# Merging the two parity halves of each K and V transfer into one, in a layer of sliding dilated attention and SwiGLU

## The chip, the cores and the metric

One core of a Trainium2 chip runs the whole layer. The metric is device time in microseconds; the time of a kernel is the median of its runs. A profiled execution gives the rows that are read here. Engines: PE multiplies matrices, DVE (VectorE) does most elementwise work, ACT (ScalarE) copies, scales and applies functions, POOL (GpSimd) does next to nothing here, and SP issues the transfers (DMA), which run on 16 DMA engines.

## The reference

A transformer layer on one sequence of S = 2048 positions, D = 640 channels, float32, with 32 heads of 20 channels. Each position attends to 8 positions of the past, two apart.

```
h  = x  + attention(layernorm(x), wqkv, wo)
h2 = h  + (silu(layernorm(h) @ w_gate) * (layernorm(h) @ w_up)) @ w_down      # F = 1728
...
# attention
W, dil = 8, 2
idx  = pos[:, None] - dil * arange(W)[None, :]        # the positions a query sees
kg   = k[:, :, idx, :] ;  vg = v[:, :, idx, :]
logits = einsum("bhsd,bhswd->bhsw", q, kg) * Dh ** -0.5   # masked where idx < 0
o    = einsum("bhsw,bhswd->bhsd", softmax(logits), vg)
```

## The kernel before

The sequence is cut into 4 blocks of 512 positions (b) and the heads into 4 groups of 8 heads, 160 channels (g). A pair (b, g) is a unit; there are 16. Because a query sees every second position only, positions of even and odd parity never meet in the attention. The 128 partitions hold it so: partitions 0 to 63 are one parity, 64 to 127 the other, and each partition owns 4 neighbouring positions of its parity.

The work of a unit:

- `qkv(b, g)` computes Q, K and V on PE into PSUM banks (L696). ACT evicts them (L703) into the staging tile `st`.
- SP stores them to DRAM: K to `ksc`, V to `vsc`, Q to `qsc`. `ksc` and `vsc` have the shape [4 groups, 2 parities, 1031 rows, 160]; a row is a position of one parity, and the first 7 rows are a halo of zeros, written once at the start by `zero_halo` (L460). Each of K and V is stored in two transfers (`put`, L716), one for each parity, from 64 partitions each.
- `att_load(b, g)` loads them again, so that each partition gets its own 4 positions and the 7 before them: 11 rows, 1760 elements, 7040 bytes, overlapping with its neighbour's. Each of K and V is loaded in two transfers (`ld`, L752), one for each parity, to 64 partitions each, into one of three slots of the tile `kv`, in turn: K of unit 0, V of unit 0, K of unit 1 and so on.
- DVE multiplies Q by the windows of K (L767) and reduces (L773); after the softmax it multiplies by the windows of V (L808), adds up (L817) and transposes (L824). The result is stored to `osc` in small transfers (L830).

Beside the attention of later units, PE computes the output projection (L901) and the feed-forward layer of earlier blocks (L989, L1004; L1158 and L1405 in the last blocks, where products are shared between blocks). The FFN weights come from DRAM (L951, L980), are split by ACT (L970) and DVE (L965) into a high and a low part, since each product is made in three passes, and the low parts are stored in the first block and loaded again in later ones (`lsc`, L980 and L975).

All steps are listed with `P.add(engine, cost, function, reads, writes, ...)`, and their order on each engine is written out as a table, `ORDER`, of (engine, first step, count). Waits follow from what each step reads and writes: a step waits for the steps that wrote what it reads, and for those that still use what it overwrites. All transfers but eight are issued by SP, one after the other in the order of the table; a transfer whose data isn't ready holds up those behind it. The names of the reads and writes of K and V carry the parity: `K{g}{par}` in DRAM and `fakv{par}` in the tile.

Of the kernel before, what the change touches and what calls it, by code (L numbers as in the profile page):

```python
# [19 lines left out]
NB, NJ, NG, NC = 4, 4, 4, 5  # L20
GC = D // NG
# [298 lines left out]
def nb(chunks, size):  # L320
    return (chunks / 16 * 0.042 + chunks * size / 435e3) * RATE
# [1286 lines left out]
```

## Time and profile before

| what | us |
|---|---|
| median of 3 runs | 842.3 |
| the runs | 841.67, 842.3, 843.37 |
| the profiled execution's own time | 845.17 |
| its span, first to last instruction | 843.4 |
| PE busy | 835.2 (99%) |
| DVE busy | 744.5 (88%) |
| ACT busy | 426.3 (51%) |

The page of the profile gives the busy time of each engine, then the span in 40 slices with the busy share of each in tenths; PEclk is PE's granted clock and DMA the mean share of the 16 DMA engines that is busy. Rows of transfers name target and source, the number of issues, the size of one and the median time from its issue to its landing. A row of a tile's answer gives the duration of an instruction (least, median, greatest, in ns; for SP it is the issue alone) and the first and last start in us. In a row of a stage the first figure is the stage's length, then comes each engine's busy time, the granted clock, the DMA share and the GB/s moved.

### The profile page before, as it was taken

The numbers are of one execution on the slowest core, as the hardware profiler recorded it, in microseconds if no ns is written. First come the engines' busy times: TensorE is split into PE (matmuls) and PEld (weight loads), VectorE is DVE, ScalarE is ACT, GpSimd is POOL, SyncE is SP. The second block draws the span as 40 slices with busy tenths as digits, with TensorE's granted clock in tenths as the row PEclk, the third lists the DMA queues.
The fourth block names the chain that finished last, engine by engine and source line by source line (L and its number), as shares of the span: only waits on it lengthen the run. The fifth ranks groups of instructions, "written<-read, shape, count | busy, mean of one in ns | idle before, by whom it ended". The sixth has DMA issues, their size and how long they took to land. (4 is left out here: it accounts for less than half of the span.)

```text
span 843.4 us, 11052 instructions
## 1 busy us (share of the span) xinstructions
PE 835.2 (99%) x4049; PEld 717.4 (85%) x4049; DVE 744.5 (88%) x934; ACT 426.3 (51%) x774; POOL 3.4 (0%) x14
## 2 busy tenths in 40 slices
PE   8999999999999999999999999999999999999998
PEld 7888888889888888888888888888888888888998
DVE  6599999999999999999999999996797676576996
ACT  7966476244873343567345347554464323335451
POOL 0000000000000000000000000000000000000000
PEclk9999999999999999999999999999999999999999
DMA  7988977678788898877999989977522133475002
GB/s 250 261 214 239 271 177 195 186 209 234 175 246 250 270 272 289 229 237 234 299 288 304 261 242 270 257 281 274 167 78 100 57 113 100 156 256 222 0 33 93
DMA packets 89877, 174.88 MB, mean 207 GB/s; under 512 B 33744, under 2 KB 53200, under 8 KB 89056
## 3 DMA queue, kind: packets, MB, share of 16 engines
q1 hardware_dynamic: 88416, 173.53, 67.7%
q10 hardware_dynamic: 1408, 0.66, 0.3%
q8 instruction: 31, 0.51, 0.2%
q14 instruction: 22, 0.18, 0.1%
HBM read 126.04 MB, written 46.80 MB: 205 GB/s over the span
## 5 line engine op out<-in xcount | busy, mean ns | idle before, releaser
L989 PE MATMUL bank<-shb,rb 128*128 128x512 f32 x930 | 227.0, 390 | 1.4 <-DVE fa L1028 0.7
L989 PEld LDWEIGHTS bank<-shb,rb 128*128 128x128 f32 x930 | 173.2, 188 | 38.4 <-DVE fa L1028 2.1
L1004 PE MATMUL bank<-rb,acts 128*128 128x512 f32 x464 | 121.4, 391 | 0.0
L1004 PEld LDWEIGHTS bank<-rb,acts 128*128 128x128 f32 x464 | 86.4, 188 | 17.3
L767 DVE TENSOR_TENSOR pq<-kv,pq 128x2560 f32<-128x2560 f32 x32 | 90.2, 2819 | 3.2 <-DMA pq<-qsc 1.9
L817 DVE TENSOR_TENSOR pq<-pq 128x1280 f32<-128x1280 f32 (+2 forms) x96 | 89.6, 934 | 2.2
L808 DVE TENSOR_TENSOR pq<-kv,pq 128x2560 f32<-128x2560 f32 x32 | 90.3, 2821 | 1.3 <-DMA kv<-vsc 0.7
L773 DVE TENSOR_REDUCE pq<-pq 128x128 f32<-128x2560 f32 x32 | 90.1, 2814 | 0.2
L703 ACT ACTIVATE st<-bank,fa 128x480 f32<-128x480 f32 (+3 forms) x120 | 50.4, 475 | 43.2 <-PE bank L696 40.8
L901 PE MATMUL bank<-ra 128*128 128x320 f32 x360 | 55.9, 309 | 0.9 <-ACT fa L904 0.9
L901 PEld LDWEIGHTS bank<-ra 128*128 128x128 f32 x360 | 54.2, 188 | 2.7 <-ACT fa L904 1.3
L970 ACT CAST rb<-fa 128x1280 fp32r<-128x1280 f32 (+1 forms) x35 | 42.5, 1217 | 25.2 <-DMA fa<-in_ffn_dram 20.0
L696 PE MATMUL bank<-ra,sha 128*128 128x480 f32 (+2 forms) x240 | 53.6, 380 | 0.0
L696 PE MATMUL bank<-rb,sha 128*128 128x512 f32 (+1 forms) x240 | 52.6, 378 | 0.0
L696 PE MATMUL bank<-ra,shb 128*128 128x512 f32 (+1 forms) x240 | 52.0, 378 | 0.0
L696 PE MATMUL bank<-rb,shb 128*128 128x512 f32 (+1 forms) x230 | 50.8, 379 | 0.0
L696 PEld LDWEIGHTS bank<-ra,shb 128*128 128x128 f32 x240 | 45.0, 188 | 6.5
L696 PEld LDWEIGHTS bank<-rb,sha 128*128 128x128 f32 x240 | 44.9, 188 | 6.4
L696 PEld LDWEIGHTS bank<-ra,sha 128*128 128x128 f32 x240 | 44.5, 188 | 6.6 <-ACT sha L643 0.2
L696 PEld LDWEIGHTS bank<-rb,shb 128*128 128x128 f32 x230 | 42.9, 188 | 6.3
L965 DVE TENSOR_TENSOR rb<-fa,rb 128x640 fp32r<-128x640 f32 (+1 forms) x54 | 43.4, 818 | 1.3 <-DMA lsc<-rb 0.7
L1027 ACT ACTIVATE fa<-bank 128x512 f32<-128x512 f32 x34 | 20.3, 598 | 42.4 <-PE bank L989 38.4
(211 smaller groups left out, 1264.8 us busy)
## 6 DMA issues: line engine op xcount, KB each, us to landing
fa<-in_ffn_dram SPq DMA_DIRECT2D x35, 960.0 KB, 7.1
kv<-ksc SPq DMA_DIRECT2D x32, 440.0 KB, 6.7
kv<-vsc SPq DMA_DIRECT2D x32, 440.0 KB, 7.4
rb<-lsc SPq DMA_DIRECT2D x17, 640.0 KB, 5.8
lsc<-rb SPq DMA_DIRECT2D x13, 640.0 KB, 6.0
rb<-lsc SPq DMA_DIRECT2D x19, 320.0 KB, 6.8
ksc<-st SPq DMA_DIRECT2D x32, 160.0 KB, 3.7
vsc<-st SPq DMA_DIRECT2D x32, 160.0 KB, 3.1
```

The costliest lines, as they stand in the source:

```text
L696: T.matmul(banks[bk][:, 0:n], l, r_(wq(g, w, c) + shift, n), start=(p, c) == first_mm, stop=(p, c) == last_mm)
L703: P.add("ACT", act(m) + 0.06, lambda: A.activation(stage_t()[:, o : o + NJ * m].rearrange("p (t j c) -> p t j c", j=NJ, c=w)[:, :, j, :], ...
L767: P.add("DVE", dve(2560), lambda: V.tensor_tensor(pq(PROD, 2560).rearrange("p (j w c) -> p j w c", j=2, w=W), window(ko, 2 * jp), pq(qo + ...
L773: P.add("DVE", dve(2560), lambda: V.tensor_reduce(logits(lo)[:, :, 16 * jp : 16 * jp + 16].rearrange("p h n -> p n h"), pq(PROD, 2560).rea ...
L808: V.tensor_tensor(pq(PROD, 2560).rearrange("p (j n d) -> p j n d", j=2, d=DH), bass.AP(tensor=v.tensor, offset=v.offset, ap=[list(v.ap[0]) ...
L817: V.tensor_add(dst(v), v[:, :, 0:m, :], v[:, :, m : 2 * m, :])
L901: T.matmul(banks[bk][:, 0:320], l, r_(m, 320), start=p == 0 and c == 0, stop=p == 2 and c == NC - 1)
L965: low(640, lambda E, o=o: E.tensor_sub(ws(t, lo + o, 640)[p0:], fa[p0:, raw + o : raw + o + 640], ws(t, hi + o, 640)[p0:].bitcast(F32)), [ ...
L970: P.add("ACT", act(n), lambda: A.copy(ws(wt, gu, n), f(raw, n)), r=[rf(raw, n)], w=[rws(wt, gu, n)], prio=PR["fh"])
L989: T.matmul(banks[bk], ws(wt, gu + 1280 * w + wid * c + col, 128), x(a, c), start=p == 0 and c == 0, stop=p == 2 and c == NC - 1)
L1004: T.matmul(banks[k], l, m, start=first and p == 0, stop=stop and p == len(passes) - 1)
L1027: P.add("ACT", act(512), lambda: A.activation(f(so, 512), banks[5], AF.Silu), r=[pb(5)], w=[rf(so, 512)], prio=0, table="silu")
```

## The change

Each of a unit's K and V is stored in one transfer from all 128 partitions, and loaded in one to all 128. The pattern in DRAM then has the parity as its first dimension, of size 2, ahead of the 64 partitions of a parity. The names of reads and writes lose the parity in DRAM, and a load writes both halves of its slot. The bytes moved, the rows (2560 bytes in a store, 7040 in a load) and all arithmetic stay as they are.

```
-            def put(par, dst, o):
+            def put(dst, o):
                 Q.dma_start(
-                    dst[g, par, 7 + 256 * b : 7 + 256 * b + 256, :].rearrange("(r j) c -> r (j c)", j=NJ),
-                    stage_t()[64 * par : 64 * par + 64, o : o + 640],
+                    dst[g, :, 7 + 256 * b : 7 + 256 * b + 256, :].rearrange("a (r j) c -> a r (j c)", j=NJ),
+                    stage_t()[:, o : o + 640],
                 )
...
-                for par in range(2):
-                    P.add("SP", 0.65, lambda par=par, dst=dst, o=o: put(par, dst, o), r=[("ab", o, o + 640)],
-                          w=[(f"{nmd}{g}{par}", 1000 + 256 * b, 1256 + 256 * b)], prio=PR["kvs"], nbytes=nb(64, 2560))
+                P.add("SP", 0.65, lambda dst=dst, o=o: put(dst, o), r=[("ab", o, o + 640)],
+                      w=[(f"{nmd}{g}", 1000 + 256 * b, 1256 + 256 * b)], prio=PR["kvs"], nbytes=nb(128, 2560))
...
-                for par in range(2):
-                    def ld(dst=dst, o=o, par=par):
-                        a = dst[g, par, 256 * b, :]
-                        Q.dma_start(kv_t()[64 * par : 64 * par + 64, o : o + 1760],
-                                    bass.AP(tensor=a.tensor, offset=a.offset, ap=[[640, 64], [1, 1760]]))
-                    lo_r = 0 if b == 0 else 1000 + 256 * (b - 1)
-                    P.add("SP", 0.45, ld, r=[(f"{nmd}{g}{par}", lo_r, 1000 + 256 * (b + 1))], w=[(f"fakv{par}", o, o + 1760)], prio=PR["atl"], nbytes=nb(64, 7040))
+                def ld(dst=dst, o=o):
+                    a = dst[g, 0, 256 * b, :]
+                    Q.dma_start(kv_t()[:, o : o + 1760],
+                                bass.AP(tensor=a.tensor, offset=a.offset, ap=[[SEQ * GC, 2], [640, 64], [1, 1760]]))
+                lo_r = 0 if b == 0 else 1000 + 256 * (b - 1)
+                P.add("SP", 0.45, ld, r=[(f"{nmd}{g}", lo_r, 1000 + 256 * (b + 1))], w=[("fakv0", o, o + 1760), ("fakv1", o, o + 1760)], prio=PR["atl"], nbytes=nb(128, 7040))
```

The table `ORDER` is written anew. It lists the same steps for PE (816), DVE (857), ACT (633) and POOL (41), in another order on each; SP has 487 steps instead of 551. The loads of K and V come at about the same places among PE's steps: the last one, V of the last unit, after 432 of PE's 816 steps instead of 433. In some units of blocks 2 and 3 the K of the next unit is loaded ahead of the V of this one.

More of the change, by code (lines that the diff above doesn't have):

```diff
@@ L467, in program @@
                 "SP", 0.07, lambda t=t: zero_halo(t), r=[rpq(PROD, 1120)],
-                w=[(f"{nm}{g}{a}", 0, 7) for g in range(NG) for a in range(2)], prio=6, nbytes=36e3,
+                w=[(f"{nm}{g}", 0, 7) for g in range(NG)], prio=6, nbytes=36e3,
             )
```

452 rows, old and new, of the table ORDER are left out of this document.

## The prediction

> **What bounds the kernel now.** I read the page first, for its shares and its DMA table, then the tiles that the change moves, then the engines and the DMA by stage, and last the count of DMA packets at the start.
>
> ```profile
> span 843.4 us, 11052 instructions
> PE 835.2 (99%) x4049; PEld 717.4 (85%) x4049; DVE 744.5 (88%) x934; ACT 426.3 (51%) x774; POOL 3.4 (0%) x14
> PEclk9999999999999999999999999999999999999999
> DMA  7988977678788898877999989977522133475002
> ...
> kv<-ksc SPq DMA_DIRECT2D x32, 440.0 KB, 6.7
> kv<-vsc SPq DMA_DIRECT2D x32, 440.0 KB, 7.4
> rb<-lsc SPq DMA_DIRECT2D x17, 640.0 KB, 5.8
> ...
> ksc<-st SPq DMA_DIRECT2D x32, 160.0 KB, 3.7
> vsc<-st SPq DMA_DIRECT2D x32, 160.0 KB, 3.1
> ```
>
> PE is busy 835.2 of 843.4 us at an undiminished granted clock, so PE sets the time, and a change of the transfers can win no more than the other 8.2 us. It can lose much more: the DMA engines are busy in seven to nine tenths of most slices of the first two thirds.
>
> The answers for the tiles kv and ksc show where the K and V transfers lie (first and last start), and the engines by stage show what else goes on there.
>
> ```profile
> L752 SPq DMA_DIRECT2D kv<-ksc x32: 445/492/988, 27.7 to 504.2; - x32
> L752 SPq DMA_DIRECT2D kv<-vsc x32: 444/462/934, 40.4 to 521.5; - x32
> L716 SPq DMA_DIRECT2D ksc<-st x32: 445/524/1482, 24.5 to 247.5; - x32
> ```
>
> ```profile
> core 0: us, PE busy (x) PEld busy (x) DVE busy (x) ACT busy (x) POOL busy (x), PEclk, DMA share, GB/s
> 24.00:250.00 226.00, 226.00 (x1117) 199.18 (x1116) 213.67 (x212) 137.67 (x299) 0.00 (x0) 1.00 0.81 220
> 250.00:542.00 292.00, 289.72 (x1367) 243.62 (x1366) 284.65 (x296) 144.47 (x220) 0.73 (x2) 1.00 0.87 264
> 542.00:843.40 301.40, 297.83 (x1476) 256.47 (x1474) 231.46 (x391) 127.51 (x219) 1.51 (x5) 1.00 0.40 140
> ```
>
> From 24 to 542 us all 64 loads and all 64 stores of K and V are made. PE loses 2.3 us in that stage (292.00 less 289.72), and DVE, which does the attention, is busy 498 of 518 us. In all this the transfers stay hidden. After 542 us no K or V moves, and the change touches nothing but the order.
>
> **What the change does to one transfer.** Of 128 issues 64 go: 32 loads and 32 stores. By the rows above an issue holds the SP queue some 0.46 to 0.56 us, so SP gains about 64 x 0.51 = 33 us. SP's issues are on no path; SP stands and waits for others, as the row below has it, so I cost this at nothing (if that cover were gone, the gain would still be bounded by PE's 2.3 us).
>
> ```profile
> SPq L830 <- DVE pq L824: 47.2, 16, 5.8
> ```
>
> What counts is the form of what is left. Before, a load reads 64 rows for 64 partitions: the pattern in DRAM starts with a dimension of 64. After, the DRAM pattern starts with the parity, a dimension of 2, with 64 rows inside, against 128 partitions in SBUF. The two parities lie 1031 x 160 elements apart, 64 rows only 64 x 640 (or, for the store, the same), so the dimensions cannot fold into one of 128. Nothing in the trace of before starts with a 2. The smallest are the two halo stores (L460), which start with 8. The start of the run, as far as 23.4 and 23.5 us, shows on how many engines one of these ran:
>
> ```profile
> GB/s 0 0 0 105 337 385 394 309 222 335 372 385 392 396 379 434 414 279 53 118 203 328 171 33 128 259 179 158 420 350 438 403 245 89 142 154 387 253 109 57
> DMA packets 3003, 5.74 MB, mean 245 GB/s; under 512 B 1064, under 2 KB 2098, under 8 KB 2874
> ...
> fa<-in_wqkv_dram SPq DMA_DIRECT2D x4, 480.0 KB, 4.2
> fa<-in_wqkv_dram SPq DMA_DIRECT2D x7, 240.0 KB, 5.3
> fa<-in_x_dram SPq DMA_DIRECT2D x4, 320.0 KB, 3.3
> fa<-in_x_dram SPq DMA_DIRECT2D x1, 1280.0 KB
> fa<-in_wqkv_dram SPq DMA_DIRECT2D x2, 32.0 KB, 3.3
> vsc<-pq SPq DMA_DIRECT2D x1, 35.0 KB
> ksc<-pq SPq DMA_DIRECT2D x1, 35.0 KB
> fa<-in_const_dram SPq DMA_DIRECT2D x1, 16.0 KB, 5.7
> fa<-in_wqkv_dram SPq DMA_DIRECT2D x1, 16.0 KB, 2.3
> ```
>
> ```profile
> DMA packets 3008, 5.75 MB, mean 245 GB/s; under 512 B 1064, under 2 KB 2103, under 8 KB 2879
> ```
>
> ```profile
> q10 hardware_dynamic: 1408, 0.66, 0.3%
> kv<-fa ACTq DMA_DIRECT2D x8, 80.0 KB, 2.8
> ```
>
> The last fence is the key to the count: 8 transfers of 80 KB in rows of 512 bytes are 1280 packets, and 128 more are counted, 16 for each transfer: one small packet at each engine's end. At the start, the rows below 512 bytes are the 32 KB, 32 KB, 16 KB and 16 KB transfers in rows of 128 bytes, 768 packets. Of the 1064 small packets 296 are left, and that is 18 x 16 + 8 (the number does not move between 23.4 and 23.5 us, so no transfer is halfway through its ends; three of the 22 issued have yet to finish). The transfer that starts with 8 ended on 8 engines, the others on 16. I read it so: the engines of a transfer follow the size of its outermost dimension. With a 2 ahead on the DRAM side that gives two engines, each with 64 rows. The trace allows the other reading too (the engines follow the number of rows, 128 here, and all 16 work); that is the second rival.
>
> [...]
>
> **The sum with two engines.** A whole load has 128 x 7040 = 901,120 bytes (twice the 440 KB), 450,560 on each of the two; a whole store 327,680, 163,840 on each. What does one engine carry? In the row of GB/s above, the best slices reach 434 and 438, or 27 GB/s for each of 16. The mean over the stage is lower:
>
> ```profile
> DMA packets 66211, 126.89 MB, mean 245 GB/s; under 512 B 28756, under 2 KB 41594, under 8 KB 65666
> ...
> q1 hardware_dynamic: 66178, 126.46, 84.2%
> ```
>
> That is 24 to 542 us: 245 / 16 / 0.845 (with the instruction queues' share) = 18.1 GB/s for an engine while it is busy. I take 26 for K and V: when two engines carry, the other 14 stand, and nothing competes with them, so they are nearest to the best slices. A load is then 17.3 us on both engines (16.7 at 27, 24.9 at 18.1), a store 6.3 us (6.1; 9.1). 16 units with two loads and two stores each: 16 x (34.6 + 12.6) = 755 us (728; 1086).
>
> The other transfers of the stage still run over all 16 and stand in the same queues: 126.46 MB less 28.8 (loads) and 10.5 (stores) is 87.1 MB, 5.45 MB for each engine: 202 us at 27 GB/s, 301 at 18.1, since many of them are small rows; I take the middle, 251. So the two engines have 755 + 251 = 1006 us of work in a stage that lasts 518 us now. PE's 516 us in it no longer cover that. The stage becomes DMA bound, and grows by at least 488 us if the two engines never stand idle.
>
> They will: SP issues in order, and each K load waits for the DVE to be done with the V two loads back, each store for ACT. Now the DMA engines stand 15.5% of the stage. With the same share after, the stage is 1006 / 0.845 = 1191 us, 673 more. A deeper queue at the two engines lets SP run further ahead than now, so I take the middle of 488 and 673, 580 us.
>
> Against the profiled execution, 845.2 us (1.8 beyond its span): 845 + 580 = 1425. It stands 2.9 us above the median of the runs, so 1422 for a median; I say **1420 us**. The low end, all at 27 GB/s and no idle time: 728 + 202 = 930, 412 more, 1257. The high end, all at 18.1 and no idle time: 1086 + 301 = 1387, 869 more, 1714. What is late next: a weight load that stands in line behind a K load comes 17 us later at two of its 16 engines, so PE and DVE wait for FFN weights as much as for K and V. After 542 us I take PE's 301 us as they are.
>
> **What could go otherwise.**
> 1. *The waiting PE slows down as well.* All slices show a granted clock of 1.00, because PE is never idle for long. Half fed, it need not keep that. At half clock its 516 us in the stage would be 1031, as much as the two engines' work, and two queues of about the same length that wait for each other would not overlap fully: if a fifth of the shorter stuck out (my guess), some 200 us more, 1620. Nothing in the rows of before speaks for it or against it, as PE nowhere starves. [...]
> 2. *All 16 engines carry the merged transfers.* For it: every transfer of 128 partitions here runs on 16. Then the change helps the DMA: a half load of 440 KB takes 6.7 us to land, one of 640 KB on 128 partitions (rb<-lsc above) 5.8, so halves are slow for their bytes and a whole of 880 KB might land in some 8 us instead of two times 6.7 in a row. But PE has only 2.3 us to win in the stage. Half of it won: 842.3 - 1.2 = 841 us, which is within the 0.2% (1.7 us) that the spread of the three runs, 841.67 to 843.37, can tell from no change; all of it won, with some of the 3.6 us after 542, 839 us. [...] This is the case on the other side, and it decides if the landing of a K load stays below about 9 us.
> 3. *All 16 engines, but a wait too coarse.* The load of a unit's K now waits for both halves of the store and for both halves of the buffer, and DVE for the last row of 128. If each of 32 loads came 0.5 us later to a DVE that is busy 98% of the stage, it would be 16 us, 858 us. Against it: the loads are issued well ahead, as PE's idle time shows.
>
> **Chances.** Two engines, as summed: 0.75. Two engines with a slow PE: 0.11. 16 engines and a little gain or none: 0.11 (0.07 within 0.2%, 0.04 faster). 16 engines and coarse waits: 0.03. So slower 0.89, same 0.07, faster 0.04. The first two cases together lie between 1257 and 1714, rounded to 1250 and 1720, with about 0.95 of their 0.86; the rest, 0.18, lies outside. As cases of the other sign hold little, this is also the likeliest one's range.
>
> **What would show it.** Two engines: K and V loads as x16 with 880 KB, landing in 19 us or more (17.3 and what stands ahead), stores as x16 with 320 KB in over 7 us; the mean DMA share of the stage down to about (2 x 1006 + 14 x 251) / 16 / 1100 = 0.31 while the stage doubles; PE busy near 59% of the span with the same busy time; waits of DVE for kv<-ksc and kv<-vsc, and of ACT for the FFN weights, on top of the list; and fewer small packets, as each of the 64 transfers ends on 2 engines. A fall of the granted clock in the starved slices would be the first rival. If the loads land in 9 us or less and PE stays at 99%, the reading of the outermost dimension was wrong, and with it the whole sum. If they take 19 us and the time is still below 1250, it is the overlap that I misjudged: then PE ran far ahead on work that needs no attention.

## The result, and the profile after

The changed kernel takes 1397.9 us (median; 1395.66 to 1400.54), the kernel before 843.3 in the same series: 1.657 times as long, interval 1.653 to 1.660, or 555 us more. I had said 1420, between 1250 and 1720.

The page of the changed kernel: engines, DMA, packets and transfers.

```profile
span 1394.0 us, 10981 instructions
PE 915.1 (66%) x4049; PEld 768.6 (55%) x4049; DVE 746.2 (54%) x934; ACT 421.6 (30%) x771; POOL 3.4 (0%) x14
...
PEclk9876586758587685887799797887587999999999
DMA  6221232222223221364463364543355763223701
...
DMA packets 87956, 174.86 MB, mean 125 GB/s; under 512 B 31824, under 2 KB 51280, under 8 KB 87136
...
DMA 54%; PE 26%; SPq 8%; DVE 4%; ACT 2%; issue 2%; DVEq 0%; ACTq 0%
...
kv<-ksc SPq DMA_DIRECT2D x16, 880.0 KB
kv<-vsc SPq DMA_DIRECT2D x16, 880.0 KB
```

The same bytes move (174.86 MB; 174.88 before), but the DMA engines are busy for 0.36 of the stage in which K and V move (its row is below), where it was 0.81 and 0.87, and the chain of work that ended last now runs through DMA for 54% of the span. The small packets give the number of engines. Before they were 33,744 (the page of before, "under 512 B"), after 31,824: 1920 fewer. The 64 transfers that are gone had 16 ends each, 1024. The other 896 are 64 x 14: each merged transfer ends on two engines. The line of the kernel before, for comparison:

```profile
DMA packets 89877, 174.88 MB, mean 207 GB/s; under 512 B 33744, under 2 KB 53200, under 8 KB 89056
```

What two engines carry can be seen where a K load is almost alone. This is the DMA answer of the changed kernel for 384 to 402 us, in 40 slices of 0.45 us:

```profile
DMA  6961111343211111141111111111111111111111
GB/s 137 358 243 53 47 63 47 112 134 114 83 63 47 63 47 63 47 122 67 47 63 47 63 47 47 63 47 63 47 47 63 47 63 47 47 63 47 63 47 63
...
kv<-ksc SPq DMA_DIRECT2D x1, 880.0 KB
```

The last 21 slices have 54 GB/s in the mean at one tenth of the engines' time: 27 GB/s for each of two. At that rate the 901,120 bytes of a load take 16.7 us. The times from issue to landing are longer. These are lines of the chain that ended last (start, us, what):

```profile
150.55 19.76 DMA kv<-ksc
...
315.96 31.32 DMA kv<-vsc
...
383.49 19.34 DMA kv<-ksc
...
600.05 33.55 DMA lsc<-rb
...
839.00 23.15 DMA fa<-in_ffn_dram
```

The K load of 383.49 us, the one above, landed 19.34 us after its issue, others on the chain up to 31.32 us. Transfers that are not merged are late as well: a store to `lsc` took 33.55 us and a load of FFN weights 23.15, where the medians before were 6.0 to 7.2, by size, and 7.1.

The stage of the K and V transfers, and what follows it (the last load was issued at 1053.0 us; with some 19 us to land, an estimate from the K load above, it is there by about 1072):

```profile
core 0: us, PE busy (x) PEld busy (x) DVE busy (x) ACT busy (x) POOL busy (x), PEclk, DMA share, GB/s
24.00:1072.00 1048.00, 583.19 (x2432) 483.90 (x2430) 489.94 (x496) 273.60 (x509) 0.73 (x2) 0.77 0.36 118
1072.00:1394.00 322.00, 310.26 (x1523) 267.58 (x1523) 241.54 (x400) 129.92 (x222) 1.53 (x5) 0.98 0.40 139
```

PE is busy 583 of 1048 us where it was 516 of 518, and DVE 490. No engine that computes is busy enough to be the bound. Who waited for whom (the answer on waits: total us, times, longest) names K and V, and everything that stands in line behind them:

```profile
DVE pq L759 <- DMA kv<-ksc: 134.7, 6, 42.4
ACT rb L962 <- DMA fa<-in_ffn_dram: 133.3, 13, 24.3
...
ACT st L697 <- DMA qsc<-st: 115.7, 6, 31.3
ACT st L697 <- DMA vsc<-st: 109.8, 8, 23.1
DVE pq L759 <- DMA pq<-qsc: 87.2, 7, 19.5
```

Q (qsc) and the FFN weights run over 16 engines as before (the count of small packets fits that), and are waited for about as long as K. The records of single packets in the trace (more than the pages show) tell how the load of FFN weights of 839.00 us came: 112 of its 128 rows of 7680 bytes had ended by 844.7 us; the other 16, which is two engines' share at 8 rows each, ended from 859.3 to 861.7, after the rows of the K load issued at 834.48 us, which went on until 857.7; the load of weights landed at 862.15. I read it so: these 16 rows stood behind the K load on its two engines. From 24 to 1072 us at least two packets were under way in 96.6% of the time, three or more in only 37.8%. These shares fit two engines that are hardly ever idle while the others mostly stand.

### The profile page after: what moved, and what is told of

It is laid out like the page before. It is cut to its first block, busy times and chain, and to the rows that moved or that the text cites. A ratio compares the mean times of both kernels' runs of the same rounds, so it can differ in the third digit from the quotient of the medians.

```text
span 1394.0 us, 10981 instructions
## 1 busy us (share of the span) xinstructions
PE 915.1 (66%) x4049; PEld 768.6 (55%) x4049; DVE 746.2 (54%) x934; ACT 421.6 (30%) x771; POOL 3.4 (0%) x14
## 2 busy tenths in 40 slices
DMA packets 87956, 174.86 MB, mean 125 GB/s; under 512 B 31824, under 2 KB 51280, under 8 KB 87136
## 4 chain that ended last, share of the span: by engine, by line
DMA 54%; PE 26%; SPq 8%; DVE 4%; ACT 2%; issue 2%; DVEq 0%; ACTq 0%
PE bank L1150 8%; PE bank L981 8%; DMA vsc<-st 8%; DMA rb<-lsc 7%; DMA fa<-in_ffn_dram 7%; DMA kv<-vsc 6%; DMA lsc<-rb 6%; PE bank L996 5%; DMA fa<-in_x_dram 5%; DMA ksc<-st 5%; DMA kv<-ksc 5%; DMA osc<-pq 4%; PE bank L1397 4%; SPq L710 2%; SPq L822 2%
## 5 line engine op out<-in xcount | busy, mean ns | idle before, releaser
L981 PE MATMUL bank<-shb,rb 128*128 128x512 f32 x930 | 251.8, 421 | 134.2 <-DMA rb<-lsc 63.2
L981 PEld LDWEIGHTS bank<-shb,rb 128*128 128x128 f32 x930 | 190.1, 207 | 179.6 <-DMA rb<-lsc 64.5
L996 PE MATMUL bank<-rb,acts 128*128 128x512 f32 x464 | 128.3, 406 | 32.0 <-DMA rb<-lsc 13.6
L690 PE MATMUL bank<-ra,shb 128*128 128x512 f32 (+1 forms) x240 | 65.3, 436 | 105.5 <-ACT st L697 70.3
L690 PEld LDWEIGHTS bank<-ra,shb 128*128 128x128 f32 x240 | 52.5, 223 | 117.8 <-ACT st L697 72.6
L800 DVE TENSOR_TENSOR pq<-kv,pq 128x2560 f32<-128x2560 f32 x32 | 90.2, 2819 | 46.5 <-DMA kv<-vsc 46.1
L893 PE MATMUL bank<-ra 128*128 128x320 f32 x360 | 62.2, 331 | 50.2 <-ACT fa L896 31.9
L893 PEld LDWEIGHTS bank<-ra 128*128 128x128 f32 x360 | 60.0, 207 | 52.7 <-ACT fa L896 32.7
L690 PE MATMUL bank<-rb,shb 128*128 128x512 f32 (+1 forms) x230 | 57.9, 415 | 34.1 <-ACT st L697 34.1
L690 PE MATMUL bank<-rb,sha 128*128 128x512 f32 (+1 forms) x240 | 59.7, 410 | 11.0 <-ACT st L697 9.6
L690 PEld LDWEIGHTS bank<-ra,sha 128*128 128x128 f32 x240 | 47.2, 201 | 26.1 <-ACT st L697 17.3
L547 PE MATMUL bank<-fa 128*128 128x128 f32 x80 | 15.3, 336 | 69.5 <-ACT fa L490 31.9
```

Source lines behind the costliest of these rows:

```text
L690: T.matmul(banks[bk][:, 0:n], l, r_(wq(g, w, c) + shift, n), start=(p, c) == first_mm, stop=(p, c) == last_mm)
L800: V.tensor_tensor(pq(PROD, 2560).rearrange("p (j n d) -> p j n d", j=2, d=DH), bass.AP(tensor=v.tensor, offset=v.offset, ap=[list(v.ap[0]) ...
L893: T.matmul(banks[bk][:, 0:320], l, r_(m, 320), start=p == 0 and c == 0, stop=p == 2 and c == NC - 1)
L981: T.matmul(banks[bk], ws(wt, gu + 1280 * w + wid * c + col, 128), x(a, c), start=p == 0 and c == 0, stop=p == 2 and c == NC - 1)
L996: T.matmul(banks[k], l, m, start=first and p == 0, stop=stop and p == len(passes) - 1)
```

## Experiments

My theory: the outermost dimension of the DRAM pattern, of size 2, sets two engines, and their queue sets the stage. Its rivals: the new order or the coarser waits; a transfer that walks two regions of DRAM is slow on any number of engines; a starved PE slows down and shares the bound.

**The parity inside, the rows outside** (sixteen). Order, waits, number of transfers and bytes are those of the changed kernel. Only the place of a token among the 128 partitions differs, so that the 64 can stand first in the pattern (lines shortened).

```
-  dst[g, :, 7 + 256 * b : ...].rearrange("a (r j) c -> a r (j c)", j=NJ)       # store
+  dst[g, :, 7 + 256 * b : ...].rearrange("a (r j) c -> r a (j c)", j=NJ)
-  ap=[[SEQ * GC, 2], [640, 64], [1, 1760]]                                     # load
+  ap=[[640, 64], [SEQ * GC, 2], [1, 1760]]
-  x: A_x.reshape(NB, 64, NJ, 2, D).transpose(0, 3, 1, 2, 4)                    # mask and output alike
+  x: A_x.reshape(NB, 64, NJ, 2, D).transpose(0, 1, 3, 2, 4)
```

Expected: 

> The changed kernel, its order and its 64 merged transfers kept, but with the 128 tokens of a block laid out so that partition 2r + parity takes the place of 64 x parity + r (the inputs, the mask and the output are laid out to suit; the arithmetic is the same). The DRAM pattern then starts with a dimension of 64 (the rows), and the parity, of 2, stands inside. Theory A (the size of the outermost dimension sets the number of engines, 2 in the changed kernel): all 16 engines carry K and V again, a load lands in 6 to 9 us, each transfer ends on 16 engines, and the time is that of the kernel before within 1%: 835 to 852 us. Rival B (the new order, or the coarser waits of a merged transfer, made it slow): the same as the changed kernel, 1380 to 1410 us. Rival C (a transfer that walks two regions of DRAM, or 128 rows of 7040 bytes at once, is slow on any number of engines): over 1100 us.

Measured: 841.5 us, 0.998 of the kernel before (0.996 to 1.000). Its page:

```profile
PE 833.5 (99%) x4049; PEld 717.5 (85%) x4049; DVE 742.7 (88%) x934; ACT 422.6 (50%) x771; POOL 3.4 (0%) x14
...
DMA packets 88852, 174.86 MB, mean 208 GB/s; under 512 B 32720, under 2 KB 52176, under 8 KB 88032
...
q1 hardware_dynamic: 87392, 173.53, 61.0%
...
kv<-ksc SPq DMA_DIRECT2D x16, 880.0 KB, 6.3
```

The whole 555 us are gone with the exchange of two dimensions. 32,720 small packets are 1024 fewer than before: 64 transfers fewer, and all others on as many engines as before. A K load of 880 KB lands in 6.3 us. Each transfer still covers both regions of DRAM, now row by row in turn. With whole transfers on 16 engines the order, the waits and the two regions cost nothing that shows; those rivals fall.

**The halves again, in the new order** (halves_both). Each merged step issues two transfers of 64 partitions (lines shortened).

```
-  Q.dma_start(kv_t()[:, o : o + 1760], AP(..., ap=[[SEQ * GC, 2], [640, 64], [1, 1760]]))
+  for par in range(2):
+      Q.dma_start(kv_t()[64 * par : 64 * par + 64, o : o + 1760], AP(..., ap=[[640, 64], [1, 1760]]))
   # the store alike
```

Expected: 

> The changed kernel with its order and its waits, but each merged transfer is issued as two halves of 64 partitions, one straight after the other, as the kernel before has them. Theory A: no K or V on two engines any more, so 840 to 860 us; what it differs by from the kernel before (842) is the price of the new order and the coarser waits. Rival B (order and waits): still 1300 us or more. Rival C (two regions in one transfer): as theory A, 840 to 860.

Measured: 850.7 us, 1.009 of the kernel before (1.006 to 1.013). As the theory has it; and the new order with coarse waits has a price of 8 us while the transfers are halves. How the 8 us divide between order and waits no run shows. The stages 24 to 250 and 250 to 542 of this run, and then of sixteen:

```profile
24.00:250.00 226.00, 226.00 (x1115) 198.81 (x1114) 213.85 (x213) 134.66 (x294) 0.00 (x0) 1.00 0.80 217
250.00:542.00 292.00, 287.22 (x1351) 242.09 (x1350) 280.40 (x289) 142.60 (x217) 0.73 (x2) 0.99 0.84 264
```

```profile
24.00:250.00 226.00, 226.00 (x1115) 198.97 (x1114) 213.42 (x212) 134.55 (x295) 0.00 (x0) 1.00 0.67 217
250.00:542.00 292.00, 292.00 (x1384) 247.18 (x1384) 287.18 (x297) 146.03 (x223) 0.73 (x2) 1.00 0.79 271
```

In the first stage both move 217 GB/s, but halves keep the 16 engines busy for 0.80 of the time, merged transfers for 0.67. In the second PE stands for 4.8 us with halves and not at all with merged transfers. In the same order the merged form is 9.2 us faster (841.5 against 850.7). So the idea behind a merged transfer holds as long as it keeps its 16 engines.

**One of the two merged** (loads_two, stores_two). The changed kernel with only the loads, or only the stores, on two engines; the others in halves as just shown.

Expected of the loads: 

> The changed kernel, but its stores are issued in two halves over 16 engines; only the 32 loads stay merged, on two engines. Theory A: the two engines have 32 x 17.3 = 554 us of loads, 251 us of the other transfers and 10.5 MB / 16 / 22 GB/s = 30 us of stores in a stage of 518 us, 835 us in all; 317 us more if they never idle, 470 more with the share of idle time of before, so about 1160 to 1315, middle 1240 us. Rival B: as the changed kernel, 1400 us. If the loads alone cost all of it (1390 or more), the stores' share was hidden.

Expected of the stores: 

> The changed kernel, but its loads are issued in two halves over 16 engines; only the 32 stores stay merged, on two engines. All stores lie in the first part, 24 to 250 us of the kernel before. Theory A: there the two engines have 32 x 6.3 = 202 us of stores, about 50 us of loads and 70 us of the rest, 322 us against 226 us: 96 us more without idle time, 155 with it, so 940 to 1000, middle 968 us. Rival B: as the changed kernel, 1400 us.

Measured: 1236.9 us with the loads (two timed runs, 1236.05 and 1237.66; 1.467 of the kernel before, 1.460 to 1.473) and 978.4 us with the stores (977.19 and 979.55; 1.160, 1.155 to 1.165). Against halves_both that is 386 us for 32 loads, 12.1 each, and 128 us for 32 stores, 4.0 each. Together 514 of the 547 us by which the changed kernel is above halves_both: the two nearly add up, with 33 us more when loads and stores are both merged. The small packets fit as well: 32,784 in each of these runs, 960 fewer than in the kernel before, which is 32 x 16 and 32 x 14. Both expectations (1240, 968) held.

**Eight loads only** (loads_b2). As halves_both, with the loads of block 2 merged (lines joined):

```
+  if b == 2:
+      Q.dma_start(kv_t()[:, o : o + 1760], AP(..., ap=[[SEQ * GC, 2], [640, 64], [1, 1760]])); return
```

Expected: 

> As the run halves_both, but the 8 loads of the four units of block 2 are merged and on two engines; all others stay in halves on 16. Theory A, by the rate of the run loads_two (394 us more for 32 loads, 12.3 each): 8 x 12.3 = 98 us on top of 850, 949 us. By the two engines' work in the stretch alone: 34.6 us of loads and about 22 of the rest in each unit against 36.5 now, 20 more for each of four, 930 us. A rival: a few two-engine loads disappear behind the work of PE and DVE, and the price comes only once the two queues are full all the way: 850 to 880 us.

Measured: 932.2 us (931.92 and 932.38), 81.5 above halves_both, 10.2 for each load. Even eight are not hidden: the estimate from the work of the two engines alone (930) was the right one, not the one from the rate of loads_two (949).

**Less work for PE** (pe_less). One pass of three is left out of Q, K and V, and of gate and up in the first two blocks.

```
+  if p == 1: continue          # in qkv, the low part of the activations
...
+  if b < 2 and p == 1: return  # in proj, one of three passes
```

Expected: 

> The changed kernel with one of three passes of PE left out (the one with the low part of the activations in Q, K and V, and one in gate and up of the first two blocks): 320 + 270 matmuls of some 0.39 us at full clock, 228 us less PE work of the 518 us or so in the stage of the K and V transfers, and nothing less for the DMA. If the two engines alone set the stage (theory A), 1340 to 1398 us. If a starved PE at its lower clock (0.77 on average in that stage) shares the bound, as the first rival of the prediction has it, at least 100 us less: 1300 or below.

Measured: 1397.3 us (1397.1 and 1397.44) against 1397.9. The stages of this run:

```profile
24.00:1072.00 1048.00, 471.35 (x1873) 383.26 (x1871) 489.28 (x496) 273.42 (x509) 0.73 (x2) 0.71 0.36 118
1072.00:1394.00 322.00, 307.93 (x1503) 265.33 (x1503) 241.54 (x400) 130.09 (x222) 1.53 (x5) 0.97 0.41 140
```

590 matmuls less, PE 112 us less busy, at a clock of 0.71 instead of 0.77, and the last load of V is issued at 1053.7 us instead of 1053.0, with the same DMA share. So the work and the clock of PE have no part in the bound that shows.

**The old order with merged transfers** (old_order_sixteen). As sixteen, but in the order of the kernel before; of each two halves the later one's place is kept.

Expected: 

> Merged transfers on all 16 engines (partition 2r + parity, as in the run named sixteen), but in the order of the kernel before: each merged transfer stands where the later of its two halves stood, and everything else keeps its place. Theory A with no price on the order: as sixteen, 839 to 844 us, for PE is busy some 833 us in both and stands between 6 and 8. If the new order is what won the 1.6 us of sixteen, this one comes out at 843 or more; if the faster transfers won them, at 842 or less.

Measured: 841.7 us, 0.998 (0.997 to 1.000). The two orders cannot be told apart with merged transfers on 16 engines; both have a median about 0.2% below that of the kernel before, and the upper end of the interval hardly stays below 1. If that is a gain, then it comes without the new order; whether from the faster transfers or from SP's 64 issues fewer, no run shows.

## Why the prediction was right

**Two engines.** This was the step on which all hung, read from one halo transfer with a first dimension of 8 that ended on 8 engines. From an 8 to a 2 it was an extrapolation, with a chance of 0.86 on it. It held: 64 x 14 ends fewer, and with 64 rows first the cost is gone. By the small packets a 2 in front gave two engines, the 8 of the halo eight, and 64 sixteen; what other sizes give, no run shows. The other reading, that the rows count, was rival 2; its condition was false for this kernel, while its price was about right: it had 839 to 841 us with 16 engines, and sixteen took 841.5.

**The size of a transfer.** A load was to keep two engines busy for 17.3 us. At the rate where it is nearly alone that is 16.7 us. In the packet records of the changed kernel a row of 7040 bytes took 267 ns in the median, or 26.4 GB/s, and 64 rows 17.1 us. That part stands, and so does the sign of a landing in 19 us or more.

**The rest of the queue and the idle time.** The work of the two engines was about right, their idle time was not. In the stage after, 0.36 x 16 x 1048 = 6037 engine-us were spent. K and V at 27 GB/s are 728 us on each of two (19.66 MB), where the forecast had 755; so the other transfers are (6037 - 1456) / 16 = 286 us for each engine, where it had 251. These two errors nearly cancel, which is luck: 728 + 286 = 1014 us of work against 1006. The split is an estimate; at the 26 GB/s of the forecast, K and V are 755 again and the rest 283. With the share rounded to 0.01, the rest is good to some 5 us. By 1014 the two engines were idle for 3% of the 1048 us, while the middle that I chose meant 1006 of 1098, 8%. The packet records agree with the 3%: in 96.6% of the stage at least two were under way. That idle time is the term that was too large. A static order that had left the engines 15.5% idle when PE was the bound left the two full engines hardly any. The argument for the middle, that a deeper queue lets SP run further ahead, is not shown: SP was held in its issues (last section), and the engines stayed busy all the same.

**The end.** From 542 us I took 301 us as they are. After 1072 us, 322 went by, but that moves with where one cuts. From the start of DVE's last product with V to the end of the span it is 843.4 - 566.5 = 277 us before and 1394.0 - 1118.8 = 275 after, so the tail is unchanged (L808 before is L800 after):

```profile
L808 DVE TENSOR_TENSOR pq<-kv,pq x32: 2783/2824/2827, 59.8 to 566.5; 128x2560 f32<-128x2560 f32 x32
```

```profile
L800 DVE TENSOR_TENSOR pq<-kv,pq x32: 2782/2820/2827, 115.1 to 1118.8; 128x2560 f32<-128x2560 f32 x32
```

All of the difference lies ahead of that product: its start moved by 552 us, the end of the span by 551.

**The slow PE.** The clock did fall, to 0.77 in the stage, and PE's busy time rose from 835 to 915 us, as rival 1 had it. So the sign of PE at 59% with the same busy time was off: it was 66%. In the changed kernel the granted clock was 0.50 from 216 to 226 us, where PE did nothing, and 1.00 from 504 to 514, where it was busy throughout; so the half clock of the rival is what the starved stretches show. That it would cost some 200 us did not come true: with 112 us less of PE the time did not move.

**The coarse waits**, rival 3, were to cost 16 us on 16 engines if each load came 0.5 us later. Sixteen has the coarse waits and none of that shows. The rival took DVE to be busy for 98% of the stage; by the rows it is 498 of 518 us, 96%.

**SP's issues** were costed at nothing. With 16 engines nothing speaks against that. In the changed kernel SP has 8% of the chain, see the last section; what that costs, with two engines busy anyway, no run shows.

## What to carry to other kernels

Before a transfer is widened, write down both patterns as they will be issued and look at the outermost dimension of each: a 2 in front, here the parity, took 14 of 16 engines away while every row and byte stayed the same. See whether another order of the partitions puts a larger dimension in front. Here, with 64 rows in front, the merged transfers were at least as good as the halves (841.5 us against 850.7 in the same order, and 0.998 of the kernel before). In the profile the sign is a low DMA share beside engines that wait for DMA, and the count of small packets, which gave the engines of a transfer by subtraction.

## What the runs showed of the hardware that I had not expected

SP itself was held while it issued. Before, the issue of a load of K or V took at most 0.99 us and of a K store at most 1.48; in the changed kernel, by the answers for the tiles kv and st, V loads took up to 22.0 us and K stores up to 15.4 us to issue:

```profile
L744 SPq DMA_DIRECT2D kv<-vsc x16: 500/1048/21981, 72.0 to 1053.0; - x16
```

```profile
L710 SPq DMA_DIRECT2D ksc<-st x16: 501/1516/15418, 24.8 to 584.4; - x16
```

In sixteen, with as many and as large transfers on 16 engines, no issue of a load of K or V took over 1.1 us; in loads_two and stores_two some took 6 us and more. So the holding comes with the transfers on two engines; by what mechanism, no run shows. While SP stands, it issues nothing for the 14 idle engines either.

Halves of 64 partitions cost engine time: 0.80 against 0.67 of 16 engines for the same 217 GB/s. The packet records show where much of it goes. A row of 7040 bytes in a load of K or V took 492 ns in the median in the kernel before and 493 in halves_both, but 267 in sixteen and in old_order_sixteen. The rows and their number are the same, so the time goes with the form of the transfer, 64 partitions or all 128. Why, no run shows.
